# An order by hand on ScalarE, a chunk's writes and the expert loads behind the gathers, and low parts on GpSimd

## Chip, cores and metric

The kernel runs on one core of one Trainium2 chip. The metric is device time in microseconds (us), the median of three runs. The core has five engines that matter here: PE (TensorE, matrix products), ACT (ScalarE), DVE (VectorE), POOL (GpSimd) and SP (SyncE, which here issues DMAs). Each works through its own queue in order, and they wait for each other by semaphores.

## What is computed

An attention with a cluster mask gives 1536 tokens of 512 numbers. A feed-forward block with a squared ReLU follows, and then a mixture of eight experts, each 512 to 1024 and back to 512, in which every token goes to at most one expert:

```python
h = np.maximum(x @ w_in, 0.0)
x = h * h @ w_out                                  # first block
do_compute = x @ w_skip > 0                        # tokens that are computed
xc = x[do_compute]
logits = xc @ w_gate
e_idx = np.argmax(logits, axis=1)
probs = softmax(logits)
gate_w = probs[np.arange(len(xc)), e_idx]
for e in range(8):
    h = np.maximum(xc[e_idx == e] @ w1[e], 0.0)
    y[e_idx == e] = gate_w[e_idx == e, None] * (h @ w2[e])
out = x.copy()
out[do_compute] = xc + y
```

## The kernel before

Tokens are held in 12 tiles of 128, and in 4 chunks `ch` of 3 tiles (384 tokens). Attention takes the first half of the span. The first block follows in four passes over its hidden size: `gemm1` (products in L248) makes `hps`, ScalarE takes relu (L255) and square (L256) of it, GpSimd rounds it to the high part `hh` (L134) and DVE subtracts for the low part `hl` (L258); `gemm2` (L1091) multiplies by `woh` and `wol`, and DVE adds the sum to the tile (L1099). Every operand is split into a high and a low part, and a product is three: high by high, low by high, high by low.

The routing starts before the last pass has ended. `early()` routes chunks 0 to 2, `late()` the last. `route` transposes the tiles (L823, copied by ScalarE to `xs`, L825), multiplies by the gate weights, takes the exponential on ScalarE (`ex`, L867), makes a one-hot `oh` of the best expert (L873), the rank of each token within its expert by products on PE (`rk`, L877), and from the exponentials the factor `gate` (L892 to L898), which `pay` (L900) combines with the one-hot. `ranks` compares ranks with slots (`so`, L915), `slots` makes the lists of tokens by products of `so` and `pay` (`sl`, L923, summed by DVE in L927 and L929), and `index` makes indices of them (L933).

The work of the second block is cut into nine units of 128 tokens. Units 0 and 1 belong to the fullest expert, which `choose()` (L937 to L949) finds from the counts of chunks 0 to 2: list A of unit 0 is gathered by `gather(0)` from `out` (GpSimd, L1021, `u<-out_dram,ixA`), list B of unit 1 by `gather(1)` when the last chunk is routed (`u<-xd,ixB`), the lists of the other seven by `gather(2)` and so on (`ixp`). `choose()` sets `pi`: the fullest expert is p = 0, and one of experts 0 and 1 is p = 1. `place` reads them into registers on SP, and `fetch` (L747) issues the weight loads: pieces of 512 KB, into seven staging buffers, `st` (three) and four that were tiles of x (`xc`). `half_weights` turns a piece into its high part on ScalarE (CAST, L765, `wih` or `woh`) and its low part by two subtractions (L769, `wil` or `wol`); a table by expert (ENG0, ENG1, ENG2) names the engines, 'av' for ScalarE and DVE, 'ap' for ScalarE and GpSimd. `parts` (L1029 to L1033) transposes 128 tokens and splits them (`xh`, `xl` or `hh`, `hl`); `g1` and `g2` are the two products of a unit, `products` (L1039) the loop in them, L1047 the relu between, `finish` (L1060, L1062) scales and scatters.

`base()` is the sequence of steps n on PE: n = 0 to 11 the last `gemm1`s, 12 to 23 the last `gemm2`, 24 to 27 `g1(0, 0)`, 28 to 31 `g1(0, 1)`, and so on. The table EVENTS says what is put before step n: 'e' is the next part of `early()`, 'l' of `late()`, 'c' the conversion of one weight piece, 'x' the transposes of unit 0's tokens. `between(gen, f)` runs f after the second step of gen. The order of the instructions of an engine is as written for the engines named in MANUAL (one set per stage; the stage here is the third), and set by a scheduler for the others. In the third stage PE and SP are so named. In this stage ScalarE's queue holds also two DMA issues for each tile of the last chunk, to `xd` (L819) and to `out` (L820); the second must come behind `gather(0)`, which reads `out`.

Of the kernel before, what the change touches and what calls it, by code (L numbers as in the profile page):

```python
# [10 lines left out]
I32 = mybir.dt.int32  # L11
AF = mybir.ActivationFunctionType
ALU = mybir.AluOpType
# [22 lines left out]
LOADAT = 7  # L36
PE, ACT, DVE, POOL, SP = (mybir.EngineType.PE, mybir.EngineType.Activation, mybir.EngineType.DVE,
                          mybir.EngineType.Pool, mybir.EngineType.SP)
EVENTS = ((1, 'e'), (2, 'e'), (3, 'e'), (4, 'e'), (8, 'e'), (11, 'e'), (12, 'c'), (13, 'e'), (15, 'c'),
          (16, 'cce'), (18, 'el'), (21, 'x'), (22, 'lcc'), (25, 'c'), (26, 'l'), (28, 'lc'), (30, 'l'), (34, 'll'))  # L40
ENG0 = ('av',) * 8
ENG1 = ('av',) * 8
ENG2 = ('av',) * 8
HOLD = 2
M0 = {DVE, PE, ACT, POOL}
AFTER = 0
PACE = 3
CLOSE = 0
MANUAL = ({PE, ACT, DVE, POOL}, {PE}, {PE, SP}, {PE})


@with_exitstack
def clustered_attention_moe(
# [685 lines left out]
    def stage(t):  # L739
        free.append(t[:, 0:1024].rearrange("p (c f) -> p c f", c=2))  # L740

    def fetch():

        while free and loads and loads[0][0] < len(e_reg):
            p, kind, n, c = loads.pop(0)
            st = free.pop(0)
            nc.sync.dma_start(out=st, in_=w_slice(e_reg[p], kind, n)[:, c:c + 2])  # L747
            loaded.append(st)
# [57 lines left out]
    sg, sgB, sgp, t2 = [rp.tile([128, 6, E], F32, name=nm) for nm in ("sg", "sgB", "sgp", "t2")]  # L806
    nc.vector.tensor_scalar(out=sg[:, 5], in0=rev8[:, 0], scalar1=-1.0, scalar2=float(E), op0=ALU.mult, op1=ALU.add)
    ixp, pi = [rp.tile([128, E], I32, name=nm) for nm in ("ixp", "pi")]
    sAB = [rp.tile([128, 6], F32, name=nm) for nm in ("sA", "sB")]
    gp = rp.tile([128, E], F32, name="gp")  # L810
    ixAB = [rp.tile([128, 1], I32, name=nm) for nm in ("ixA", "ixB")]
# [4 lines left out]
    def turn_x(T):  # L816

        q = nc.sync if T < NT - GT else nc.scalar
        q.dma_start(out=xdv[T // TT, T % TT], in_=x1[T])  # L819
        q.dma_start(out=outv[T // TT, T % TT], in_=x1[T])  # L820
        xps = ps_x.tile([128, KD, 128], F32, name="xps", tag="x")
        for c in range(KD):
            nc.tensor.transpose(out=xps[:, c], in_=x1[T][:, c * 128:(c + 1) * 128], identity=ident)  # L823
        xs_t[T] = rp.tile([128, KD, 128], F32, name="xs", bufs=3)
        nc.scalar.copy(out=xs_t[T], in_=xps)  # L825
# [6 lines left out]
    def route(ch):  # L832
# [52 lines left out]
            count(i + 1, GT + 1, ones16, spread(oh16[:, ch * GT + i], GT - i), stop=(i == GT - 1))  # L885
        if ch >= NC - 2:
            nc.vector.tensor_copy(out=cnt, in_=rk[:, GT])
        rke = rp.tile([128, GT, E], F32, name="rke")
        nc.vector.tensor_tensor(out=rke, in0=rk[:, 0:GT], in1=oh16[:, t_], op=ALU.mult)
        nc.vector.tensor_reduce(out=rank[:, t_], in_=rke, op=ALU.add, axis=AX.X)  # L890
# [46 lines left out]
    def choose():  # L937

        nc.vector.tensor_reduce(out=cmax, in_=cnt, op=ALU.max, axis=AX.X)
        nc.vector.tensor_scalar(out=full, in0=cnt, scalar1=cmax, scalar2=None, op0=ALU.is_equal)  # L940
        nc.vector.tensor_tensor(out=full, in0=full, in1=rev8[:, 0], op=ALU.mult)
        er = rp.tile([128, 1], F32, name="er")
        nc.vector.tensor_reduce(out=er, in_=full, op=ALU.max, axis=AX.X)
        nc.vector.tensor_scalar(out=full, in0=full, scalar1=er, scalar2=None, op0=ALU.is_equal)
        nc.vector.tensor_scalar(out=pi[:, 0:1], in0=er, scalar1=-1.0, scalar2=float(E), op0=ALU.mult, op1=ALU.add)
        nc.vector.tensor_scalar(out=pi[:, 1:2], in0=full[:, 1:2], scalar1=-1.0, scalar2=1.0,
                                op0=ALU.mult, op1=ALU.add)
        nc.vector.tensor_scalar_min(nA, cmax, 128.0)
        place(2)  # L949

    def place(n):
        while len(e_reg) < n:
            p = len(e_reg)
            e_reg.append(nc.sync.value_load(pi[0:1, p:p + 1], min_val=0, max_val=E - 1))
            if p == 0:
                fetch()

    def pick(i, sum):

# [5 lines left out]
    def early():  # L965

        for ch in range(NC - 1):
            while done[0] <= ch:
                yield
            yield from route(ch)  # L970
            so = ranks(ch)
            yield
            if ch == NC - 2:
                choose()
            slots(ch, sg, so)
            if ch == NC - 2:
                pick(0, sg)
                gather(0)
            if ch < HOLD:
                stage(xc[ch])  # L980
            if ch == NC - 2:
                so = ranks(0, nA)
            yield
        for ch in range(NC - 1):
            slots(ch, sgB, so)
            if ch < NC - 2:
                so = ranks(ch + 1, nA)
            yield

    def late():  # L990
# [3 lines left out]
        slots(NC - 1, sgB, so)  # L994
        pick(1, sgB)
        gather(1)
        for ch in range(HOLD, NC):
            stage(xc[ch])
        yield
# [6 lines left out]
            lists[p + 1] = (ixp[:, p:p + 1], gp[:, p:p + 1])  # L1006
        gather(2)
        nc.vector.tensor_copy(out=pi, in_=sgp[:, 5])
        place(E)
        yield  # L1010


# [4 lines left out]
    def gather(u):  # L1017

        xg = xgs[u % 3]
        nc.gpsimd.memset(xg, 0.0)  # L1020
        nc.gpsimd.indirect_dma_start(  # L1021
            out=xg, in_=xd if u else out, in_offset=bass.IndirectOffsetOnAxis(ap=lists[u][0], axis=0),
            out_offset=None, bounds_check=N - 1, oob_is_err=False)
# [159 lines left out]
    for u in range(1, UN):  # L1183
# [9 lines left out]
        do(g1(u, 1) if u > 1 else between(g1(u, 1), lambda: turn_h(u, 0)))  # L1193
        if u + 1 < UN:
            xp_t[u + 1] = parts(xgs[(u + 1) % 3], "x")
        do(g2(u, 0))
        turn_h(u, 1)
    do(g2(UN - 1, 1))
    finish(UN - 1)

# [65 lines left out]
```

## Time and profile before

| | us |
|---|---|
| median of three runs | 683.02 |
| lowest and highest | 680.4, 685.97 |
| the profiled execution's own time | 684.3 |
| its span | 682.5 |
| PE busy in it | 648.4 (95%) |
| DVE, ACT, POOL busy in it | 477.4 (70%), 415.7 (61%), 253.7 (37%) |

The span is the time from the first to the last instruction that the profile saw; the rest of the execution lies around it. In the rows, a time in the front column is counted from the span's start, the next number is the duration, and the bracket at a row's end says how long the engine had been idle, and what ended that. PE, DVE, ACT, POOL are engines, PEq, ACTq and so on their instruction queues. [...]

### The profile page before, as it was taken

Reading aid. Unit: us, or ns where it says so; the run is one execution under the profiler, and the core shown is the slowest. Engines: PE = TensorE matmul, PEld = TensorE weight load, DVE = VectorE, ACT = ScalarE, POOL = GpSimd, SP = SyncE. Lnnn points to the kernel's source line nnn. Section 1 sums busy time; section 2 is a strip of 40 time slices with the busy share of each in tenths; the row PEclk is TensorE's granted clock in tenths of the full one; section 3 lists DMA queues with packets and bytes.
Section 4 is the critical chain, followed back from the end, with each engine's and each line's share of the span. In section 5 each row is a group of like instructions: output and inputs, shape, how many; then the busy total and the mean of one; then the engine's idle time right before and its main releaser. Section 6 shows DMA issues by size and latency. Waiting matters only on the chain. (4 is left out here: it accounts for less than half of the span.)

```text
span 682.5 us, 11258 instructions
## 1 busy us (share of the span) xinstructions
PE 648.4 (95%) x3769; PEld 566.0 (83%) x3769; DVE 477.4 (70%) x928; ACT 415.7 (61%) x846; POOL 253.7 (37%) x329
## 2 busy tenths in 40 slices
PE   7899899999999998999999999999999797999994
PEld 6788888989898887999998999999888575888883
DVE  4787899999999999654456455522244688899950
ACT  5799889989998984544433333322323375778830
POOL 4816264544736346643343443511010103113110
PEclk9899999999999999999999999999999989999998
DMA  5867764665746100123122312101222697999900
GB/s 130 190 150 154 185 142 122 150 157 127 164 123 139 41 1 9 63 66 104 63 78 62 108 63 62 40 0 47 93 93 94 216 315 252 345 356 362 367 13 23
DMA packets 72034, 89.90 MB, mean 132 GB/s; under 512 B 32384, under 2 KB 43584, under 8 KB 71968
## 3 DMA queue, kind: packets, MB, share of 16 engines
q1 hardware_dynamic: 68096, 84.12, 42.5%
q0 software_dynamic: 1440, 3.01, 1.3%
q10 hardware_dynamic: 2432, 1.97, 0.9%
q8 instruction: 32, 0.52, 0.3%
q14 instruction: 34, 0.28, 0.1%
HBM read 62.18 MB, written 9.44 MB: 105 GB/s over the span
## 5 line engine op out<-in xcount | busy, mean ns | idle before, releaser
L578 DVE TENSOR_TENSOR pl<-pt,ph 128x384 fp32r<-128x384 f32 x192 | 103.5, 551 | 19.2 <-ACT ph L569 18.0
L255 ACT ACTIVATE r<-hps 128x384 f32<-128x384 f32 x62 | 30.5, 492 | 120.7 <-PE hps L248 115.7
L555 PE MATMUL pt<-ident,p 128*128 128x128 f32 x576 | 95.9, 276 | 3.9 <-DVE pl L578 2.8
L513 PE MATMUL sc<-B,A 80*128 80x384 f32 (+1 forms) x384 | 91.8, 361 | 2.0 <-ACT p L529 1.8
L569 ACT CAST ph<-pt 128x384 fp32r<-128x384 f32 x192 | 89.7, 481 | 6.6 <-PE pt L555 5.9
L520 DVE TENSOR_REDUCE nm<-sc 128x1 f32<-128x768 f32 x96 | 91.0, 948 | 2.5 <-PE sc L513 2.5
L258 DVE TENSOR_TENSOR hl<-r,hh 128x384 fp32r<-128x384 f32 x62 | 36.7, 591 | 76.4 <-POOL hh L134 76.0
L529 ACT ACTIVATE p<-sc,nm 128x768 f32<-128x768 f32 x96 | 87.3, 910 | 4.4 <-DVE nm L520 4.3
L555 PEld LDWEIGHTS pt<-ident,p 128*128 128x128 f32 x576 | 70.4, 141 | 18.3 <-DVE pl L578 10.9
L134 POOL TENSOR_SCALAR hh<-r 128x384 fp32r<-128x384 f32 x62 | 35.4, 571 | 134.3 <-ACT r L256 114.9
L1091 PE MATMUL acc<-woh,hh 128*128 128x512 f32 x186 | 74.3, 400 | 0.0
L1091 PE MATMUL acc<-wol,hh 128*128 128x512 f32 x186 | 73.5, 395 | 0.0
L588 PE MATMUL av<-ph,vs 128*128 128x384 f32 x192 | 73.0, 380 | 0.1
L1091 PE MATMUL acc<-woh,hl 128*128 128x512 f32 x186 | 72.9, 392 | 0.0
L513 PEld LDWEIGHTS sc<-B,A 80*128 80x128 f32 (+1 forms) x384 | 63.2, 191 | 6.3 <-ACT p L529 6.2
L588 PE MATMUL av<-pl,vs 128*128 128x384 f32 x192 | 65.2, 339 | 0.6 <-DVE pl L578 0.6
L248 PE MATMUL hps<-A,wil 128*128 128x384 f32 x184 | 61.9, 336 | 2.0 <-POOL wil L180 2.0
L248 PE MATMUL hps<-A,wih 128*128 128x384 f32 x184 | 62.4, 339 | 0.0
L248 PE MATMUL hps<-B,wih 128*128 128x384 f32 x184 | 61.9, 337 | 0.0
L164 ACT ACTIVATE u<-st 128x512 f32<-128x512 f32 x32 | 21.7, 677 | 32.9 <-DMA st<-in_moe_w_in_dram 25.6
L1091 PEld LDWEIGHTS acc<-woh,hl 128*128 128x128 f32 x186 | 35.2, 189 | 7.8
L1091 PEld LDWEIGHTS acc<-woh,hh 128*128 128x128 f32 x186 | 35.2, 189 | 5.7 <-DVE xc L1099 0.2
(260 smaller groups left out, 1484.1 us busy)
## 6 DMA issues: line engine op xcount, KB each, us to landing
xc<-in_moe_w_dram SPq DMA_DIRECT2D x34, 512.0 KB, 5.5
st<-in_moe_w_dram SPq DMA_DIRECT2D x30, 512.0 KB, 5.8
st<-in_moe_w_in_dram SPq DMA_DIRECT2D x64, 128.0 KB, 2.9
st<-in_moe_w_out_dram SPq DMA_DIRECT2D x16, 512.0 KB, 3.9
A<-hi SPq DMA_DIRECT2D x30, 192.0 KB, 3.5
B<-hi SPq DMA_DIRECT2D x30, 192.0 KB, 4.0
qn<-in_q_dram SPq DMA_DIRECT2D x16, 192.0 KB, 3.5
vn<-in_v_dram SPq DMA_DIRECT2D x16, 192.0 KB, 2.6
```

What stands on the lines that cost most here:

```text
L134: nc.gpsimd.tensor_scalar(out=o, in0=i, scalar1=1.0, scalar2=0.0, op0=ALU.mult, op1=ALU.add)
L248: nc.tensor.matmul(out=hps, lhsT=wi[w][:, c, f * 128:(f + 1) * 128], rhs=xhl[ch][a][:, c], start=(n == 0), stop=(n == 3 * KD - 1))
L255: nc.scalar.activation(out=r, in_=hps, func=AF.Relu)
L258: nc.vector.tensor_tensor(out=hl, in0=r, in1=hh.bitcast(F32), op=ALU.subtract)
L513: nc.tensor.matmul(out=sc[:, c, 0:384], lhsT=A[h][0:kk, a, t * 128:(t + 1) * 128], rhs=Bk[h][0:kk, a, c * 384:(c + 1) * 384], start=(a == ...
L520: nc.vector.tensor_reduce(out=nm_t[i], in_=sc_t[i][:, :, 0:384], op=ALU.max, axis=AX.XY, negate=True)
L529: nc.scalar.activation(out=p, in_=sc[:, :, 0:384], func=AF.Exp, bias=nm, scale=1.0, accum_out=su_t[n, c][:, t, h:h + 1])
L555: nc.tensor.transpose(out=pt[:, c], in_=p_t[i][:, n, c * 128:(c + 1) * 128], identity=ident)
L569: nc.scalar.copy(out=block(i, n)[by_pool].bitcast(F32) if by_pool else block(i, n)[0], in_=pt_t[i, n])
L578: nc.vector.tensor_tensor(out=pl, in0=pt_t.pop((i, n)), in1=ph.bitcast(F32), op=ALU.subtract)
L588: nc.tensor.matmul(out=av, lhsT=vs[:, c, 2 * h:2 * h + 2].rearrange("p x d -> p (x d)"), rhs=r[:, c], start=(c == 0 and i == 0), stop=(c = ...
L1091: nc.tensor.matmul(out=acc, lhsT=h2[a][:, i * 128:(i + 1) * 128], rhs=wo[w][:, f], start=(f == 0 and n == 0), stop=(f == NF - 1 and n == 2))
```

## The change

EVENTS is laid out anew, with the weight pieces and unit 0's transposes at other steps. ScalarE is named in the third stage's MANUAL set. The eight subtractions of the second expert's first weights (p = 1, w1) are on GpSimd (ENG1). The writes of the last chunk to `out` go from ScalarE's queue to SP's, after `gather(1)`. `choose()` moves ahead of the rank and gate work of its chunk. It sets only the first expert's register and issues up to two loads; the second expert's number goes through GpSimd behind `gather(0)` (`pi1`), and the other loads are issued after that. In the last unit the transposes of the first half of `hs` stand between the products of `g2`. Lines of the kernel after are 1 to 13 further on.

```diff
--- before.py
+++ after.py
@@ -36,17 +36,18 @@
 LOADAT = 7
 PE, ACT, DVE, POOL, SP = (mybir.EngineType.PE, mybir.EngineType.Activation, mybir.EngineType.DVE,
                           mybir.EngineType.Pool, mybir.EngineType.SP)
-EVENTS = ((1, 'e'), (2, 'e'), (3, 'e'), (4, 'e'), (8, 'e'), (11, 'e'), (12, 'c'), (13, 'e'), (15, 'c'),
-          (16, 'cce'), (18, 'el'), (21, 'x'), (22, 'lcc'), (25, 'c'), (26, 'l'), (28, 'lc'), (30, 'l'), (34, 'll'))
+EVENTS = ((1, 'e'), (2, 'e'), (3, 'e'), (4, 'e'), (8, 'e'), (11, 'e'), (13, 'e'), (16, 'e'), (18, 'el'), (20, 'c'),
+          (21, 'c'), (22, 'l'), (23, 'c'), (24, 'xc'), (26, 'l'), (27, 'c'), (28, 'l'), (29, 'c'), (30, 'l'), (32, 'c'),
+          (33, 'c'), (34, 'll'))
 ENG0 = ('av',) * 8
-ENG1 = ('av',) * 8
+ENG1 = ('ap',) * 4 + ('av',) * 4
 ENG2 = ('av',) * 8
 HOLD = 2
 M0 = {DVE, PE, ACT, POOL}
 AFTER = 0
 PACE = 3
 CLOSE = 0
-MANUAL = ({PE, ACT, DVE, POOL}, {PE}, {PE, SP}, {PE})
+MANUAL = ({PE, ACT, DVE, POOL}, {PE}, {PE, SP, ACT}, {PE})
 
 
 @with_exitstack
@@ -739,9 +740,10 @@
     def stage(t):
         free.append(t[:, 0:1024].rearrange("p (c f) -> p c f", c=2))
 
-    def fetch():
-
-        while free and loads and loads[0][0] < len(e_reg):
+    def fetch(n=len(loads)):
+
+        while free and loads and loads[0][0] < len(e_reg) and n:
+            n -= 1
             p, kind, n, c = loads.pop(0)
             st = free.pop(0)
             nc.sync.dma_start(out=st, in_=w_slice(e_reg[p], kind, n)[:, c:c + 2])
@@ -806,6 +808,7 @@
     sg, sgB, sgp, t2 = [rp.tile([128, 6, E], F32, name=nm) for nm in ("sg", "sgB", "sgp", "t2")]
     nc.vector.tensor_scalar(out=sg[:, 5], in0=rev8[:, 0], scalar1=-1.0, scalar2=float(E), op0=ALU.mult, op1=ALU.add)
     ixp, pi = [rp.tile([128, E], I32, name=nm) for nm in ("ixp", "pi")]
+    pi1 = rp.tile([128, 1], I32, name="pi1")
     sAB = [rp.tile([128, 6], F32, name=nm) for nm in ("sA", "sB")]
     gp = rp.tile([128, E], F32, name="gp")
     ixAB = [rp.tile([128, 1], I32, name=nm) for nm in ("ixA", "ixB")]
@@ -817,7 +820,8 @@
 
         q = nc.sync if T < NT - GT else nc.scalar
         q.dma_start(out=xdv[T // TT, T % TT], in_=x1[T])
-        q.dma_start(out=outv[T // TT, T % TT], in_=x1[T])
+        if T < NT - GT:
+            q.dma_start(out=outv[T // TT, T % TT], in_=x1[T])
         xps = ps_x.tile([128, KD, 128], F32, name="xps", tag="x")
         for c in range(KD):
             nc.tensor.transpose(out=xps[:, c], in_=x1[T][:, c * 128:(c + 1) * 128], identity=ident)
@@ -885,6 +889,8 @@
             count(i + 1, GT + 1, ones16, spread(oh16[:, ch * GT + i], GT - i), stop=(i == GT - 1))
         if ch >= NC - 2:
             nc.vector.tensor_copy(out=cnt, in_=rk[:, GT])
+        if ch == NC - 2:
+            choose()
         rke = rp.tile([128, GT, E], F32, name="rke")
         nc.vector.tensor_tensor(out=rke, in0=rk[:, 0:GT], in1=oh16[:, t_], op=ALU.mult)
         nc.vector.tensor_reduce(out=rank[:, t_], in_=rke, op=ALU.add, axis=AX.X)
@@ -946,14 +952,13 @@
         nc.vector.tensor_scalar(out=pi[:, 1:2], in0=full[:, 1:2], scalar1=-1.0, scalar2=1.0,
                                 op0=ALU.mult, op1=ALU.add)
         nc.vector.tensor_scalar_min(nA, cmax, 128.0)
-        place(2)
-
-    def place(n):
+        place(1, pi)
+        fetch(2)
+
+    def place(n, src):
         while len(e_reg) < n:
             p = len(e_reg)
-            e_reg.append(nc.sync.value_load(pi[0:1, p:p + 1], min_val=0, max_val=E - 1))
-            if p == 0:
-                fetch()
+            e_reg.append(nc.sync.value_load(src[0:1, 0:1] if n == 2 else src[0:1, p:p + 1], min_val=0, max_val=E - 1))
 
     def pick(i, sum):
 
@@ -970,12 +975,15 @@
             yield from route(ch)
             so = ranks(ch)
             yield
-            if ch == NC - 2:
-                choose()
             slots(ch, sg, so)
             if ch == NC - 2:
                 pick(0, sg)
                 gather(0)
+
+                nc.gpsimd.tensor_scalar(out=pi1, in0=ixAB[0], scalar1=0.0, scalar2=None, op0=ALU.mult)
+                nc.gpsimd.tensor_tensor(out=pi1, in0=pi1, in1=pi[:, 1:2], op=ALU.add)
+                place(2, pi1)
+                fetch()
             if ch < HOLD:
                 stage(xc[ch])
             if ch == NC - 2:
@@ -994,6 +1002,8 @@
         slots(NC - 1, sgB, so)
         pick(1, sgB)
         gather(1)
+        for T in range(NT - GT, NT):
+            nc.sync.dma_start(out=outv[T // TT, T % TT], in_=x1[T])
         for ch in range(HOLD, NC):
             stage(xc[ch])
         yield
@@ -1006,7 +1016,7 @@
             lists[p + 1] = (ixp[:, p:p + 1], gp[:, p:p + 1])
         gather(2)
         nc.vector.tensor_copy(out=pi, in_=sgp[:, 5])
-        place(E)
+        place(E, pi)
         yield
 
 
@@ -1193,8 +1203,11 @@
         do(g1(u, 1) if u > 1 else between(g1(u, 1), lambda: turn_h(u, 0)))
         if u + 1 < UN:
             xp_t[u + 1] = parts(xgs[(u + 1) % 3], "x")
-        do(g2(u, 0))
-        turn_h(u, 1)
+        if u + 1 < UN:
+            do(g2(u, 0))
+            turn_h(u, 1)
+        else:
+            do(between(g2(u, 0), lambda: turn_h(u, 1)))
     do(g2(UN - 1, 1))
     finish(UN - 1)
 
```

On ScalarE, at the end of the last gemm1, the relu and square of the first block (L255 and L256, after: L256 and L257), the exponential of the third chunk (ex) and the first weight casts (wih) stood like this before:

```order
L255 ACTIVATE r<-hps 128x384
L256 ACTIVATE r<-r 128x384
L867 ACTIVATE ex<-ex 128x24
L255 ACTIVATE r<-hps 128x384
L256 ACTIVATE r<-r 128x384
L255 ACTIVATE r<-hps 128x384
L256 ACTIVATE r<-r 128x384
L819 DMA xd<-xc_91 128x512
L765 CAST wih<-st 128x1024
L820 DMA out_dram<-xc_91 128x512
L765 CAST wih<-st 128x1024
L825 COPY xs<-xps 128x512
```

and stand like this after:

```order
L256 ACTIVATE r<-hps 128x384
L257 ACTIVATE r<-r 128x384
L256 ACTIVATE r<-hps 128x384
L257 ACTIVATE r<-r 128x384
L871 ACTIVATE ex<-ex 128x24
L256 ACTIVATE r<-hps 128x384
L257 ACTIVATE r<-r 128x384
L822 DMA xd<-xc_91 128x512
L829 COPY xs<-xps 128x512
L767 CAST wih<-st 128x1024 x2
L822 DMA xd<-xc_91 128x512
L829 COPY xs<-xps 128x512
```

The exponential stands one relu and one square later, and between the casts now stand copies of xs and no write to `out`.

On DVE, the chain from the exponential's first reader (gate) to pay of the third chunk began like this before (pay comes eight instructions after these):

```order
L892 TENSOR_REDUCE gate<-ex 128x3
L873 TENSOR_TENSOR oh_3989<-oh_6475,sel 128x24
L893 TENSOR_SCALAR gate<-gate 128x3
L903 TENSOR_TENSOR cum_3990<-cum_3990,oh_3989 128x8
L258 TENSOR_TENSOR hl<-r,hh 128x384
L894 RECIPROCAL gate<-gate 128x3
L903 TENSOR_TENSOR cum_3990<-cum_3990,oh_3989 128x8
L896 CAST vals<-gate 128x3
L903 TENSOR_TENSOR cum_3990<-cum_3990,oh_3989 128x8
L898 TENSOR_TENSOR gate<-gate,vals 128x3
L887 COPY cnt<-rk 128x8
L889 TENSOR_TENSOR rke<-rk,oh_3989 128x24
```

and begins like this after (pay comes eight instructions after these, too):

```order
L898 TENSOR_REDUCE gate<-ex 128x3
L918 TENSOR_SCALAR rkb<-rank,nA 128x3
L259 TENSOR_TENSOR hl<-r,hh 128x384
L949 TENSOR_REDUCE er<-full 128x1
L899 TENSOR_SCALAR gate<-gate 128x3
L921 TENSOR_TENSOR so<-slot,rkb 128x384
L950 TENSOR_SCALAR full<-full,er 128x8
L951 TENSOR_SCALAR pi<-er 128x1
L900 RECIPROCAL gate<-gate 128x3
L952 TENSOR_SCALAR pi<-full 128x1
```

The next step of gate now stands behind an hl, and the reciprocal behind a comparison (so) and the small instructions of choose().

On GpSimd, around the gathers of list A (ixA) and list B (ixB), hh being the last high parts of the first block, the order was this before:

```order
L1020 MEMSET u 128x512
L134 TENSOR_SCALAR hh<-r 128x384 x21
L1021 DMA u<-out_dram,ixA 128x512
L1021 DMA u<-xd,ixB 128x512
L1021 DMA l_5821<-xd,ixp 128x512
```

and is this after (pi is the second expert's number, wil the low parts of the second expert's w1):

```order
L135 TENSOR_SCALAR hh<-r 128x384 x20
L1031 DMA u<-out_dram,ixA 128x512
L983 TENSOR_SCALAR pi_4007<-ixA 128x1
L135 TENSOR_SCALAR hh<-r 128x384
L984 TENSOR_TENSOR pi_4007<-pi_4007,pi 128x1
L771 TENSOR_TENSOR wil<-xc_88,wih 128x512 x2
L771 TENSOR_TENSOR wil<-xc_89,wih 128x512 x2
L771 TENSOR_TENSOR wil<-st,wih 128x512 x3
L1031 DMA u<-xd,ixB 128x512
L1031 DMA l_5822<-xd,ixp 128x512
L771 TENSOR_TENSOR wil<-st,wih 128x512
```

One hh of the first block moved behind the first gather's issue, and seven subtractions stand ahead of the second gather.

On PE, around unit 0's transposes (xps<-ident,u) and its first products (hps<-wih,xh), the order was this before:

```order
L1091 MATMUL acc<-wol,hh 128x512
L1091 MATMUL acc<-woh,hl 128x512
L1029 MATMUL xps<-ident,u 128x128 x4
L1091 MATMUL acc<-woh,hh 128x512
L1091 MATMUL acc<-wol,hh 128x512
L1091 MATMUL acc<-woh,hl 128x512
L823 MATMUL xps<-ident,xc_91 128x128 x4
L829 MATMUL lps<-wgs,xs 128x9 x4
L1091 MATMUL acc<-woh,hh 128x512
L1091 MATMUL acc<-wol,hh 128x512
L1091 MATMUL acc<-woh,hl 128x512
L1091 MATMUL acc<-woh,hh 128x512
```

and is this after:

```order
L833 MATMUL lps<-wgs,xs 128x9 x4
L1101 MATMUL acc<-woh,hh 128x512
L1101 MATMUL acc<-wol,hh 128x512
L1101 MATMUL acc<-woh,hl 128x512
L1101 MATMUL acc<-woh,hh 128x512
L1101 MATMUL acc<-wol,hh 128x512
L1101 MATMUL acc<-woh,hl 128x512
L1039 MATMUL xps<-ident,u 128x128 x4
L1049 MATMUL hps<-wih,xh 128x512
L1049 MATMUL hps<-wil,xh 128x512
L1049 MATMUL hps<-wih,xl 128x512
```

The transposes of u moved behind the last products of the first block, directly ahead of the first products that read them.

## Rows read from the trace of the kernel before

**Rows 1.** The page's second part: granted clock of PE in 40 slices of the span.

```profile
PEclk9899999999999999999999999999999989999998
```

**Rows 2.** Waits of PE from 500 us on: total, times, longest.

```profile
PE xps L1029 <- DMA u<-out_dram,ixA: 2.8, 1, 2.8
PE acc L1039 <- ACT hh L1032: 2.6, 2, 1.9
PE sl L923 <- DVE pay L900: 1.5, 2, 1.0
PE hps L1039 <- ACT xh L1032: 0.7, 1, 0.7
PE xps L823 <- ACT xs L825: 0.6, 1, 0.6
```

**Rows 3.** Windows of 4 us: length, busy time of each engine, clock, DMA share, GB/s.

```profile
544.00:548.00 4.00, 3.40 (x16) 2.97 (x15) 3.30 (x6) 4.00 (x7) 0.00 (x0) 0.63 1.04 378
548.00:552.00 4.00, 4.00 (x11) 3.08 (x11) 2.60 (x5) 2.45 (x3) 0.00 (x0) 0.52 0.98 349
...
560.00:564.00 4.00, 2.51 (x14) 1.55 (x14) 4.00 (x15) 3.17 (x5) 0.00 (x0) 1.00 0.91 314
```

**Rows 4.** Timeline of PE: start, duration, engine, line, operation, idle time before.

```profile
532.11 0.24 PE L923 MATMUL sl<-pay,so 128*128 128x40 bf16 x3 [0.56 <-DVE pay L900]
...
558.48 0.17 PE L877 MATMUL rk<-oh,tri 128*128 128x24 bf16 x1 [0.49 <-DVE oh L873]
...
579.28 0.50 PE L1039 MATMUL acc<-woh,hh 128*128 128x512 f32 x1 [1.89 <-ACT hh L1032]
...
670.53 0.50 PE L1039 MATMUL acc<-woh,hh 128*128 128x512 f32 x1 [0.68 <-ACT hh L1032]
```

**Rows 5.** Timeline of ACT (ScalarE), same columns.

```profile
528.56 0.21 ACT L867 ACTIVATE ex<-ex 128x24 f32<-128x24 f32 x1
...
530.38 0.53 ACT L256 ACTIVATE r<-r 128x384 f32<-128x384 f32 x1
...
543.48 1.05 ACT L765 CAST wih<-st 128x1024 fp32r<-128x1024 f32 x1 [4.23 <-DMA u<-out_dram,ixA]
...
555.29 0.60 ACT L1047 ACTIVATE hs<-hps 128x512 f32<-128x512 f32 x1 [0.74 <-PE hps L1039]
...
562.66 0.59 ACT L1032 CAST hh<-xps 128x512 fp32r<-128x512 f32 x1
...
577.70 1.05 ACT L765 CAST wih<-st 128x1024 fp32r<-128x1024 f32 x1 [2.12 <-DMA st<-in_moe_w_dram]
```

**Rows 6.** Timeline of DVE (VectorE), same columns.

```profile
531.47 0.59 DVE L900 TENSOR_TENSOR pay<-oh,vals 128x120 bf16<-128x120 bf16 x1
...
533.08 0.55 DVE L915 TENSOR_TENSOR so<-slot,rkb 128x384 bf16<-128x384 f32 x1
```

**Rows 7.** Timeline of POOL (GpSimd), same columns.

```profile
530.98 0.94 POOL L134 TENSOR_SCALAR hh<-r 128x384 fp32r<-128x384 f32 x1 [1.74 <-ACT r L256]
534.13 0.51 POOL L134 TENSOR_SCALAR hh<-r 128x384 fp32r<-128x384 f32 x1 [2.21 <-ACT r L256]
535.26 1.56 POOL L1021 DMA_INDIRECT u<-out_dram,ixA  x1 [0.61 <-DVE hl L258]
565.56 1.38 POOL L1021 DMA_INDIRECT u<-xd,ixB  x1 [28.74 <-DMA xc<-in_moe_w_dram]
```

**Rows 8.** Lines L180 and L769, the subtractions: min, median, max in ns.

```profile
L180 POOL TENSOR_TENSOR wil<-u,wih x16: 1279/1311/1712, 94.9 to 431.7; 128x512 fp32r<-128x512 f32 x16
...
L769 DVE TENSOR_TENSOR wil<-xc,wih x34: 667/681/694, 547.8 to 646.3; 128x512 fp32r<-128x512 f32 x34
```

**Rows 9.** Timeline of GpSimd and DVE, where they meet and where not.

```profile
371.33 1.31 POOL L180 TENSOR_TENSOR wol<-u,woh 128x512 fp32r<-128x512 f32 x1
...
371.66 1.26 DVE L166 TENSOR_SCALAR u<-u 128x512 f32<-128x512 f32 x1
...
400.23 0.42 DVE L166 TENSOR_SCALAR u<-u 128x512 f32<-128x512 f32 x1
```

## The prediction

> **What bounds the kernel.** I read the page's first two parts first: PE is busy 95% of the span (table above), so what counts is where it waits or runs slowly. The granted clock [rows 1] is at or near full everywhere but in the slice from 546 to 563 us. The waits of PE from 500 us to the end [rows 2] list the stalls there: 2.8 us for the gathered tokens u (list A), 2.6 for hh (two waits), 1.5 for pay (two), 0.7 for xh, 0.6 for xs. [...]
>
> So the region 528 to 582 us decides, and the end of the last unit. All times below are against the profiled execution, 684.3 us with a span of 682.5, some 1.3 above the median of 683.02; I apply differences to the median.
>
> **What the change removes.** (1) The transposes of u go behind the rest of the last gemm2 on PE (the order fence on PE), nine products and another tile's transposes later: the 2.8 us [rows 2] go. (2) ScalarE's write to `out` waited on the gather at its queue's head; the cast behind it shows 4.23 us of idle time, ended by u [rows 5]. It held xs, for which PE waited 0.6; with the write on SP this goes. (3) The clock: if its fall follows the gather's stall, 3.2 us. (4) The 1.89 us before 579.28: there a cast of weights waited 2.12 us for its load and stood ahead of hh [rows 5]; the new ScalarE order has hh ahead of that cast. (5) The last unit's transposes of hs move between the products of gemm2, where the 0.68 us before 670.53 [rows 4] and a shorter wait behind it go: 0.8 as an estimate. Sum: 2.8 + 0.6 + 3.2 + 1.9 + 0.8 = 9.3 us.
>
> **What it adds.** (a) ScalarE's exp for the third chunk now stands behind one more relu and square (order fence on ScalarE). Before, it began at 528.56, and the square ahead of which it stood ended at 530.91 [rows 5]: exp ends near 531.1 instead of 528.77, 2.36 later. Its readers, gate to pay, were through at 532.06 [rows 6], 3.3 us behind it, as the last of 20 DVE instructions. Now 18 stand there, and the third is an hl that waits for GpSimd's hh, which ended at 531.92 [rows 7]; gate's chain goes on behind it (order fence on DVE). From 531.92: hl and one comparison at 0.55 [rows 6], 13 small ones at some 0.1, an estimate, and pay 0.3 give 534.6. PE waits for pay at 532.11 already [rows 4], so the delay of 2.6 us is all new stall: 2.6 (1.9, if other work hid the small ones, to 3.3).
> (b) On GpSimd the gather's issue, 1.56 us [rows 7], and two small instructions now stand ahead of the last hh of the last gemm1, which began at 534.13 before it. I take 0.2 us off for slack, an estimate: 1.35 (0 to 1.6).
> (c) The transposes of u stand directly ahead of the first products that read xh and xl. The same pattern for the second list costs 0.7 us for xh [rows 2]; xl is a subtraction of 0.68 [rows 8] behind others on DVE, another 1.1 (0 to 1.4): 1.85.
> (d) The last chunk's one-hot now stands on DVE behind the first two subtractions of w2 and hl. Their cast follows hs on ScalarE. From hs at 555.29 (0.60 us [rows 5]): cast 1.05, two subtractions 1.3, four small ones 0.6, hl 0.6, oh 0.2 gives 559.7; PE got rk at 558.48 [rows 4]: 1.2 (0 to 1.5).
> (e) gather(1) stands behind seven of GpSimd's eight subtractions (order fence on GpSimd). The last of their casts stands behind hh, which began at 562.66 [rows 5]: 562.66 + 0.59 + 1.05, one more cast 1.05, one subtraction 1.31 [rows 8] is 566.65, against an issue at 565.56 [rows 7]: 1.1 (0 to 2).
> (f) Weight loads: the second and later ones now wait on SP for a register that GpSimd makes behind the gather's issue, so they start some 5 us later, an estimate from (a) and the 1.56. The casts of g1(0,0)'s pieces should still come 1 to 2 us before PE reaches them: nothing; if that cover is gone, 1 to 2 us. The out-writes on SP stand behind gather(1), between loads that run a unit ahead: nothing.
> Sum: 2.6 + 1.35 + 1.85 + 1.2 + 1.1 = 8.1. Without more, the change gains 1.2 us.
>
> **GpSimd's subtractions.** One 128x512 subtraction takes 1.31 us on GpSimd and 0.68 on DVE [rows 8], and eight leave DVE. But one instruction of DVE's that met such a subtraction took 1.26 us instead of 0.42 (371.66 against 400.23, with the GpSimd row at 371.33 [rows 9]): it was held 0.84. Seven of the eight fall between the last chunk's logits and ixB, where PE waits for DVE's chain (1.5 us for pay already [rows 2]). The lower bound is 0: the freed 8 x 0.68 us of DVE could even repay it. The upper is their whole length, 7 x 1.31 = 9.2. I take four that hold something for which PE waits: 4 x 0.84 = 3.4, about half of the seven, since the chain itself stops for PE and ScalarE between its parts. Then -1.2 + 3.4 = +2.2: **685.2 us**.
>
> [...]
>
> **Rivals.**
> B, as designed: the waits go and (a), (b), (d), (e) are hidden, only (c) stays: -9.3 + 1.85 = -7.4, 675.6. For it: every removed stall stands in a row. Against: DVE is busy all of 560 to 564 [rows 3], so a later exp or a later cast is late for PE.
> [...]
> D, the clock falls somewhere else: the gap made by (a) is 0.56 + 2.6 = 3.2 us, longer than the 2.8 that came before the fall, while 1.89 had none. Then the 3.2 stay lost: 685.2 + 3.2 = 688.4.
> E, it does not do what it says: the counter of fetch is overwritten inside its loop, so fetch(2) issues one load where two were named. No stall hangs on that second load before the gather, so this leaves the time at the forecast's.
>
> **Numbers.** Chances: forecast with E 0.42, B 0.20, C 0.18, D 0.20. A measurement of this kernel tells about 1% (6.8 us) from no change. Faster than 676.2: most of B, 0.16, and 0.01 of the rest, 0.17. Slower than 689.9: 0.09 of C, 0.09 of D, 0.07 of the forecast's own spread, 0.25. Same: 0.58. The forecast's own range is 681 to 689; with half of B and most of C the range is 676 to 691.
>
> **What would show it.** Right: no wait for u<-out_dram; a wait for pay of about 3.2 us near 532; waits for hh of GpSimd and for xh of the first unit; rk and sl waits of over 2 us together with GpSimd's subtractions, and DVE instructions of the chain at 0.8 us and more beside them; the acc wait of 1.89 and the end's 0.68 gone. Wrong: pay no later than before (the exp term), a full clock through 528 to 560 with waits under 4 us in sum (B), or two slices at a clock under 0.8 (D).

## The result and the profile after

The changed kernel took 694.09 us (median of four runs, 691.34 to 696.09) against 683.31 for the kernel before (median of four, too): the ratio is 1.0148, with a 95% interval of 1.0116 to 1.0179. It is slower by 1.5%, and above the range of the prediction. The profiled execution took 691.34 us with a span of 689.6, 7.0 more than the one of before; it is the quickest of the four.

The waits of PE from 500 us to the end, after (total, times, longest):

```profile
PE sl L929 <- DVE pay L906: 7.7, 2, 4.6
PE rk L881 <- DVE oh L877: 1.7, 1, 1.7
PE rk L881 <- DVE sel L876: 1.5, 1, 1.5
PE hps L1049 <- ACT xh L1042: 1.4, 2, 0.7
PE hps L1049 <- DVE xl L1043: 0.9, 2, 0.7
PE acc L1101 <- POOL hh L135: 0.7, 1, 0.7
```

Of the rows of before [rows 2] the waits for u of list A, for hh from ScalarE and for xs are gone, as forecast. In their place stand 7.7 us for pay and 3.2 for rk. Before, beside the rows shown ahead, the chain of the last chunk cost PE only this (same view, kernel before):

```profile
PE rk L877 <- DVE oh L873: 0.5, 1, 0.5
PE sl L923 <- DVE sgB L929: 0.5, 1, 0.5
PE xps L1029 <- DMA u<-xd,ixB: 0.4, 1, 0.4
```

The timeline of PE shows where the waits lie:

```profile
535.23 0.24 PE L929 MATMUL sl<-pay,so 128*128 128x40 bf16 x3 [3.07 <-DVE pay L906]
...
539.10 0.50 PE L1101 MATMUL acc<-woh,hh 128*128 128x512 f32 x1 [0.74 <-POOL hh L135]
...
548.88 0.50 PE L1049 MATMUL hps<-wih,xh 128*128 128x512 f32 x1 [0.68 <-ACT xh L1042]
...
560.31 0.17 PE L881 MATMUL rk<-oh,tri 128*128 128x24 bf16 x1 [1.65 <-DVE oh L877]
...
570.08 0.28 PE L929 MATMUL sl<-pay,so 128*128 128x40 bf16 x3 [4.64 <-DVE pay L906]
...
677.65 0.40 PE L1049 MATMUL acc<-woh,hl 128*128 128x512 f32 x1
```

The first wait for pay (3.07 us at 535.23) belongs to the third chunk, and answers to the 0.56 at 532.11 [rows 4]. The one of 4.64 belongs to the last chunk. The 1.89 us ahead of 579.28 and the 0.68 ahead of 670.53 of before [rows 4] have no counterpart any more. The last product ends at 678.05, before at 673.85:

```profile
673.46 0.39 PE L1039 MATMUL acc<-woh,hl 128*128 128x512 f32 x1
```

The windows of 4 us (busy time of PE, PEld, DVE, ACT, POOL, then the granted clock as a share of the full one, DMA share, GB/s):

```profile
536.00:540.00 4.00, 3.25 (x16) 1.90 (x14) 1.95 (x8) 1.01 (x2) 2.15 (x4) 1.00 0.52 173
...
560.00:564.00 4.00, 3.69 (x14) 2.98 (x14) 3.97 (x12) 1.85 (x3) 3.43 (x2) 0.66 0.05 18
564.00:568.00 4.00, 1.43 (x7) 0.90 (x6) 4.00 (x9) 2.74 (x4) 2.81 (x2) 0.92 0.97 316
568.00:572.00 4.00, 1.50 (x9) 1.22 (x10) 4.00 (x18) 0.00 (x0) 2.20 (x3) 0.51 0.38 142
572.00:576.00 4.00, 4.00 (x13) 3.14 (x12) 0.65 (x8) 1.04 (x1) 3.08 (x3) 0.64 0.28 76
```

Before, the clock was 0.63 and 0.52 at 544 to 552 [rows 3]. After, it is 1.00 in both of these windows and below 1 from 560 to 576. What was lost is, as an estimate, the busy time by the missing share: 3.69 x 0.34 + 1.43 x 0.08 + 1.50 x 0.49 + 4.00 x 0.36 = 3.5 us.

DVE's chain of the last chunk, after, and GpSimd's subtractions beside it (both timelines; the first number is the start, the second the duration):

```profile
557.10 1.25 DVE L870 SCALAR_TENSOR_TENSOR oh<-ex,rev 128x24 f32<-128x24 f32 x1
...
562.76 0.17 DVE L896 TENSOR_REDUCE rank<-rke 128x3 f32<-128x24 f32 x1
562.85 1.16 DVE L902 CAST vals<-gate 128x3 bf16<-128x3 f32 x1
...
564.65 0.17 DVE L902 CAST vals<-gate 128x3 bf16<-128x3 f32 x1
...
565.26 1.76 DVE L771 TENSOR_TENSOR wol<-st,woh 128x512 fp32r<-128x512 f32 x1
566.94 1.23 DVE L902 CAST vals<-gate 128x3 bf16<-128x3 f32 x1
...
568.68 1.33 DVE L906 TENSOR_TENSOR pay<-oh,vals 128x120 bf16<-128x120 bf16 x1
```

```profile
556.88 2.65 POOL L771 TENSOR_TENSOR wil<-xc,wih 128x512 fp32r<-128x512 f32 x2 [17.69 <-ACT wih L767]
560.56 3.43 POOL L771 TENSOR_TENSOR wil<-xc,wih 128x512 fp32r<-128x512 f32 x2 [1.03 <-DVE gate L899]
565.19 4.69 POOL L771 TENSOR_TENSOR wil<-st,wih 128x512 fp32r<-128x512 f32 x3 [1.20 <-ACT wih L767]
```

A step of the one-hot (oh) took 1.25 us, a cast of three numbers a partition (vals) 1.16 and 1.23, a subtraction 1.76 instead of 0.68 [rows 8], pay 1.33. Each began while GpSimd was in a subtraction; the same cast at 564.65, when GpSimd was in none, took 0.17. The reduction at 562.76 began beside a subtraction, too, and took 0.17, so not every instruction beside a subtraction took longer. GpSimd's subtractions took longer in turn, 1.7 us each in the second pair (3.43 for two) instead of 1.31 [rows 8].

The last difference stands at the end. From the page of the profile, before and after, the span and the packets of the second queue that it calls "instruction" (q14):

```profile
span 682.5 us, 11258 instructions
...
q14 instruction: 34, 0.28, 0.1%
```

```profile
span 689.6 us, 11269 instructions
...
q14 instruction: 35, 0.29, 0.1%
```

And the wait of SP's queue for PE's at the last line of the program (the waits of SP from 670 us on), before and after:

```profile
SPq L1261 <- PEq L1261: 3.0, 2, 2.5
```

```profile
SPq L1274 <- PEq L1274: 5.7, 2, 5.1
```

Before, the last product ended at 673.85 and the span 8.65 us later; after, at 678.05 and 11.55 us later. So 2.9 of the 7.0 us come behind the last product.

### The profile page after: what moved, and what is told of

Its sections match the earlier page's. It is cut to its first block, busy times and chain, and to the rows that moved or that the text cites. A ratio compares the mean times of both kernels' runs of the same rounds, so it can differ in the third digit from the quotient of the medians.

```text
span 689.6 us, 11269 instructions
## 1 busy us (share of the span) xinstructions
PE 648.2 (94%) x3769; PEld 565.3 (82%) x3769; DVE 480.9 (70%) x920; ACT 416.4 (60%) x846; POOL 263.5 (38%) x339
## 5 line engine op out<-in xcount | busy, mean ns | idle before, releaser
L256 ACT ACTIVATE r<-hps 128x384 f32<-128x384 f32 x62 | 30.4, 491 | 126.1 <-PE hps L249 118.7
L556 PEld LDWEIGHTS pt<-ident,p 128*128 128x128 f32 x576 | 70.0, 140 | 18.5 <-DVE pl L579 10.8
```

The costliest lines, as they stand in the source:

```text
L256: nc.scalar.activation(out=r, in_=hps, func=AF.Relu)
L556: nc.tensor.transpose(out=pt[:, c], in_=p_t[i][:, n, c * 128:(c + 1) * 128], identity=ident)
```

## The experiments

All ratios are to the kernel before, run beside the kernel on the same chip, with 95% intervals; the times of different experiments come from different chips, so ratios are compared.

**e1: low parts back on DVE.** The kernel after with

```diff
-ENG1 = ('ap',) * 4 + ('av',) * 4
+ENG1 = ('av',) * 8
```

> The kernel after with p=1's eight low-part subtractions of w1 back on DVE. Theory 1 (GpSimd's subtractions hold DVE's rank chain): the waits of 1.47 and 1.65 us for rk shrink to about 1.5 together, the 4.64 us for the last chunk's pay to 1 to 1.5, and the half-speed stretches behind them (some 3.4 us lost at 561 to 575) go; in all 6 to 9 us: 685 to 688. Theory 2 (what costs is ScalarE's order by hand, with exp and the casts late, and the later loads): the waits stay within 1 us of what they are, 692 to 695.

Measured: 688.63 us beside 685.19 for before, 1.0049 (1.0016 to 1.0081). The last chunk's wait for pay gave way to one of 1.44 us for sgB; rk cost 2.4 us instead of 3.1, and 2.69 us for u of list B came in. So by the ratios GpSimd's part of the loss is 0.9 to 1.0%, and half a per cent is left. This part holds the subtractions that run and those in a loop that doesn't; e5 parts the two. The slow stretches did not go, as theory 1 expected: in this profile the clock was 0.50 from 536 to 540, behind a wait of 3.08 us for the third chunk's pay, and 0.50 from 576 to 580, behind the wait for list B.

**e2: the same subtractions in the kernel before**, ENG1 as in after, nothing else.

> The kernel before with only the eight subtractions moved to GpSimd. Theory 1: rk and pay waits grow by 3 to 6 us around 556 to 570, and the clock may fall a second time there: 687 to 692. Theory 2: no change within 2 us of 683.3, or a gain of up to 2 since DVE is relieved.

Measured: 693.38 us, 1.0128 (1.0091 to 1.0165). This one line, which also reaches the loop that doesn't run, loses nearly as much as the whole change. Theory 2 falls as the main cause.

**e3 and e4: ScalarE's order left to the scheduler**, in after and in e1's kernel.

```diff
-MANUAL = ({PE, ACT, DVE, POOL}, {PE}, {PE, SP, ACT}, {PE})
+MANUAL = ({PE, ACT, DVE, POOL}, {PE}, {PE, SP}, {PE})
```

> The kernel after with ScalarE's order left to the scheduler again in that stage (all else as after). [...] Theory 2: nearly the whole loss goes, 683 to 687.

> Both undone: subtractions on DVE and ScalarE's order left to the scheduler; what is left is the new EVENTS, choose() early, the loads and out-writes behind the gathers and the end's transposes. Theory 1: about 681 to 685, the waits for u and for the casts gone and the chain's waits small. Theory 2: the same as e3 within 1 us, 683 to 687.

Measured: e3 693.57 us, 1.0127 (1.0092 to 1.0162); e4 683.94 us, 0.9994 (0.9964 to 1.0024). With GpSimd's subtractions the order by hand makes no difference that shows; without them it costs, by the ratios, the half per cent that e1 had left, though the two intervals overlap. e3's profiled execution (686.64 us) lies far from its other four (692.28 to 693.93), so its waits say little of them; the third chunk's pay waited 1.59 us in it. What remains of the change in e4 (EVENTS, choose() early, loads and writes behind the gathers, the end) is worth nothing on balance: its profile has no wait for u of list A, but 2.40 us for xh, 1.92 for rk and 1.19 for GpSimd's hh.

**e5: the skipped loop as before.** These inputs never enter the loop for overfull experts, but the loop holds p = 1's conversions too, so the change had put 64 subtractions there on GpSimd. The kernel after with

```diff
-                (nc.vector if eng[1] == "v" else nc.gpsimd).tensor_tensor(
+                (nc.vector if eng[1] == "v" or src is not None else nc.gpsimd).tensor_tensor(
```

> The kernel after, with the low parts on DVE only in the loop for overfull experts, which these inputs skip: GpSimd has 64 instructions fewer to jump over, and nothing else changes. In the kernels with GpSimd's subtractions the span ends 11.2 to 11.6 us behind PE's last product, in those without 8.6. Theory 3 (the longer skipped code costs one more fetch of instructions at the end): the end comes 8.6 us behind the last product, 2.9 less than after: about 691. Rival (the tail is chance, or belongs to the scatter): 11.5 us, the time as after, 694.

Measured: 688.95 us, 1.0053 (1.0019 to 1.0087). The last product ended at 677.99 and the span at 686.6: 8.6 us, as theory 3 says. By the ratios the gain, 0.8 to 1.0%, is more than the 2.9 us of the tail. No executed instruction differs, yet in this profile the last chunk's pay took 0.28 us, though GpSimd had three subtractions from 567.22 on (timelines of DVE and GpSimd, then of PE):

```profile
567.84 0.28 DVE L906 TENSOR_TENSOR pay<-oh,vals 128x120 bf16<-128x120 bf16 x1
```

```profile
567.22 4.55 POOL L771 TENSOR_TENSOR wil<-st,wih 128x512 fp32r<-128x512 f32 x3 [1.93 <-ACT wih L767]
```

```profile
568.18 0.24 PE L929 MATMUL sl<-pay,so 128*128 128x40 bf16 x3 [1.66 <-DVE pay L906]
```

The wait was 1.66 instead of 4.64: pay took 0.28 and the cast ahead of it (at 567.17) 0.17 here, 1.33 and 1.23 in after. It brought nothing in this profile, since 2.04 us for u of list B came in and the last product ended with after's to 0.06 us: the 3.0 us between the two profiled executions are the tail alone. What the rest of the gain in the ratio is stays open. Beside e1 (1.0049), which has none of these subtractions on GpSimd, run or not, e5's 1.0053 says one thing more: in the kernel after, the eight subtractions that run cost nothing that could be told within these intervals (0.3% to each side), and what e1 gained goes with the code that is not run.

**e6: the exponential earlier.** After, with the third chunk's exp one relu and square earlier on ScalarE:

```diff
+        if ch == NC - 2:
+            yield
         rk = ps_l.tile([128, GT + 1, E], F32, name="rk", tag="l")
```

(and one more 'e' in EVENTS, at step 6).

> The kernel after with one more stop in route, so that the third chunk's exp stands on ScalarE one relu and square earlier, as before the change; PE's and GpSimd's order is as after. If exp's place makes the first pay wait: it falls from 3.07 to under 1 us, and 2 to 2.5 us go: about 691.5. If choose() ahead of gate on DVE makes it: it stays over 2 us, 694.

Measured: 691.36 us, 1.0062 (1.0045 to 1.0079). PE's timeline:

```profile
539.32 0.24 PE L931 MATMUL sl<-pay,so 128*128 128x40 bf16 x3 [1.61 <-DVE pay L908]
...
543.62 0.49 PE L1103 MATMUL acc<-woh,hh 128*128 128x512 f32 x1 [1.18 <-POOL hh L135]
```

The wait fell from 3.07 to 1.61 us, not under 1: about half belongs to exp's place. In the rest, choose()'s instructions and one more hl now stand between gate and pay on DVE; no run moves choose() alone, so that it is theirs is not shown. Part went into a longer wait for hh. The ratio is 0.7 to 0.9% below that of after, more than these waits account for; the last chunk's pay still cost 5.19 us there, so the interval and the chain's chance may carry the rest. It stays open.

**e7 and e8: parts of the change alone in the kernel before.** e7 moves the last unit's transposes between its products and the out-writes to SP; e8 also moves unit 0's transposes to step 24.

```diff
-EVENTS = ... (18, 'el'), (21, 'x'), (22, 'lcc'), (25, 'c') ...
+EVENTS = ... (18, 'el'), (22, 'lcc'), (24, 'x'), (25, 'c') ...
```

> The kernel before with only the last unit's transposes moved between the products, and the last chunk's out-writes on SP behind gather(1). Theory: the wait of 0.68 us at the end and that of 0.60 for xs go, the casts of the first weights start earlier, the waits for u and for hh stay: 1 to 2 us faster than before, ratio 0.997. Rival (the freed ScalarE only shifts the stall into the wait for u): 0 to 1 us.

> The same with the transposes of u at step 24 as in after, and the weight pieces where before has them. If moving the transposes takes the wait for u away without a new one: that wait 0, xh and xl waits of 1.4 to 2.4, and if the clock's fall follows the gap for u it goes too: 4 to 6 us faster than before, ratio 0.992 to 0.994. If the clock falls all the same and xh and xl take the gain: within 1 us of the kernel without it.

Measured: e7 684.81 us, 0.9974 (0.9948 to 1.0001); e8 688.08 us, 1.0014 (0.9984 to 1.0043). e7's profile lost the two waits it was to lose, and has 3.61 us for u and 3.30 for rk. In e8 the wait for u is gone and one of 3.43 for xh stands at 549.23 instead, and the clock was 0.50 to 0.74 from 548 to 564. Moving the consumer behind other work moved the stall to the next consumer; the two ratios' intervals overlap.

**e9: skipped code alone.** The kernel before with 64 subtractions on GpSimd in the loop that is not entered; in the executed part every engine's order is that of before.

```diff
-                (nc.vector if eng[1] == "v" else nc.gpsimd).tensor_tensor(
+                (nc.vector if src is None or kind else nc.gpsimd).tensor_tensor(
```

> The kernel before with 64 subtractions put on GpSimd in the loop for overfull experts alone, which these inputs skip: not one executed instruction differs from before. Theory 3 (skipped code costs a fetch at the end): the span ends 11.5 us behind PE's last product instead of 8.6, and the ratio is 1.004 (2.9 of 685). Rival: 8.6 us and a ratio within 0.001 of 1.

Measured: 689.36 us, 1.0065 (1.0038 to 1.0092). The last product, the page's rows, and SP's wait at the end:

```profile
672.96 0.39 PE L1039 MATMUL acc<-woh,hl 128*128 128x512 f32 x1
```

```profile
span 684.4 us, 11258 instructions
...
q14 instruction: 35, 0.29, 0.1%
```

```profile
SPq L1261 <- PEq L1261: 5.5, 2, 4.9
```

As many instructions ran as before (11258), the last product ended at 673.35, before's time to half a microsecond, and the span 11.05 us later; there is one packet more on q14. In each of the seven profiles with the extra code for GpSimd in that loop (after, e2, e3, e6, e9, e11, e15) the tail is 11.0 to 11.7 us, in each of the eleven without it 8.6 to 8.8. The packets of q14, in the fourteen of these profiles whose page gives them, are 34 in the nine without the code and 35 in the five with it, but for e15 with 36. So the code goes with 2.4 (e9) to 2.9 us (after) of tail and with one packet more; that the packet fills this time, no row shows. By the ratio e9 lost some 4.4 us, 2 more than its tail; what these are stays open.

**e10: the executed subtractions alone.** The kernel before with ENG1 of after and e5's line.

> The kernel before with GpSimd's eight subtractions in the executed part alone, the skipped loop as before. Theory 1 (the rank chain on DVE is held): what e2 showed without its tail, ratio 1.0075 to 1.010, tail 8.6 us, waits for oh and pay of 2 to 4 us each. Rival, which e5 and e1 suggest by their nearly equal ratios (the held chain costs nearly nothing, the tail and chance are the rest): 1.000 to 1.004.

Measured: 690.87 us, 1.0106 (1.0070 to 1.0142), tail 8.6 us. PE's timeline:

```profile
559.83 0.17 PE L877 MATMUL rk<-oh,tri 128*128 128x24 bf16 x1 [2.60 <-DVE oh L873]
...
568.65 0.28 PE L923 MATMUL sl<-pay,so 128*128 128x40 bf16 x3 [3.68 <-DVE pay L900]
```

Against 0.49 for rk [rows 4] and 0.96 for pay before, the chain costs 4.8 us more, and the clock fell to 0.67 and 0.52 behind these two gaps. Theory 1 stands in the kernel before; in the kernel after, e1 and e5 give its subtractions no price of their own. e9's and e10's prices add to 1.7%, e2's is 1.28: within the intervals the two make up the third.

**e11 and e12: after once more, and its subtractions on another matrix.** e12 puts the second expert's w2 on GpSimd instead of w1 (ENG1 = ('av',) * 4 + ('ap',) * 4, and e5's line).

> The kernel after, unchanged, beside the others: if its ratio is 1.013 to 1.016 as first measured, e5's gain of over 0.9% is more than its 2.9 us of tail, and GpSimd's meeting with pay (4.64 us against 1.66 in e5's profile) is the rest. If it is near 1.0095, e5's gain is the tail alone.

> The kernel after with GpSimd doing the low parts of the second expert's w2 instead of w1: as many subtractions, but behind gather(1) and the last chunk's rank chain, and the skipped loop on DVE. If what costs is the place (the chain), it is as e1, ratio 1.003 to 1.006, with waits for pay and oh like e1's. If the number costs, 1.009 or more.

Measured: e11 693.8 us, 1.0136 (1.0103 to 1.0168), which repeats the first result; e12 689.71 us, 1.0085 (1.0060 to 1.0109). e12's profile has e1's waits (3.08, 1.44, 2.55 us) and a span of 687.7 against e1's 687.6, but its ratio lies between the two expectations: place against number is not settled by it.

**e13 and e14: filling the gaps.** e13 is the kernel before with ten extra products ahead of unit 0's transposes; their result is overwritten. e14 is e7 with eleven there and eight ahead of the last chunk's rank products.

```diff
+        for _ in range(fill):
+            w = wparts[steps[-1][0]][1][0]
+            nc.tensor.matmul(out=tps, lhsT=w[:, 0, 0:128], rhs=w[:, 0], start=True, stop=True)
         for c in range(4):
             nc.tensor.transpose(out=tps[:, c], in_=src[:, c * 128:(c + 1) * 128], identity=ident)
```

> The kernel before with ten extra products of 128x512 on PE ahead of unit 0's transposes (their result is overwritten): at 0.23 us each they fill 2.3 of the 2.8 to 3.6 us in which PE waited for u. If the half speed at 545 to 551 follows PE's idle time, it goes, and the time falls by about 3 us, ratio 0.995 to 0.997. If it follows something else, it stays, and the ratio is 0.999 to 1.002.

> e7's kernel with eleven such products ahead of unit 0's transposes and eight ahead of the last chunk's rank products, where its profile shows waits of 3.61 and 3.30 us, each followed by a slower stretch. If the slow stretches follow the idle time, both go and with them 3 to 6 us: ratio 0.990 to 0.994, faster than both kernels. If not, 0.996 to 1.000 as e7.

Measured: e13 684.15 us, 0.9984 (0.9957 to 1.0011); e14 682.32 us, 0.9968 (0.9948 to 0.9989). e13's timeline of PE and windows:

```profile
539.49 2.43 PE L1030 MATMUL xps<-woh 128*128 128x512 f32 x10
543.02 0.66 PE L1032 MATMUL xps<-ident,u 128*128 128x128 f32 x4 [1.10 <-DMA u<-out_dram,ixA]
```

```profile
544.00:548.00 4.00, 3.40 (x22) 2.71 (x20) 3.41 (x6) 4.00 (x7) 0.00 (x0) 1.00 0.98 361
548.00:552.00 4.00, 3.30 (x21) 2.65 (x20) 4.00 (x8) 3.45 (x5) 0.00 (x0) 1.00 0.98 349
```

The wait for u is 1.10 us instead of 2.8, and the stretch that ran at 0.63 and 0.52 before [rows 3] runs at 1.00. So at this place the fall does follow the idle time; over the twelve runs the mean clock was 0.987 to 0.995, against 0.980 to 0.993 for before beside them. But in the profile a later fall came (0.77 and 0.80 at 576 to 584, where PE stood idle for 1.33 us of the first window), and the ratio doesn't part from 1. In e14 no window is below 1.00:

```profile
544.00:548.00 4.00, 3.61 (x24) 3.26 (x25) 3.00 (x5) 2.82 (x4) 0.00 (x0) 1.00 1.05 407
548.00:552.00 4.00, 3.84 (x24) 3.06 (x23) 3.72 (x7) 2.85 (x5) 0.00 (x0) 1.00 1.05 391
...
560.00:564.00 4.00, 2.74 (x19) 2.09 (x19) 4.00 (x15) 2.29 (x4) 0.00 (x0) 1.00 1.03 368
```

It is the one kernel faster than both, by 0.3% against the kernel before; 0.6 to 1.0% was expected. How much of that is the products' and how much e7's edits, the two ratios don't tell; the clock is the products'.

**e15 and e16: the same in after and in e4**, eight products ahead of rk and five ahead of the last chunk's sl.

> The kernel after with eight extra products on PE ahead of the last chunk's rank products (waits of 1.47 and 1.65 us in its profile) and five ahead of its sl products (4.64 us); no other engine's order differs. If a fall of the clock follows idle time: the slow stretch at 561 to 565 (1.6 us lost) goes, the one behind the longer gap may stay; 1.5 to 3 us less, ratio 1.009 to 1.012 instead of 1.0136 to 1.0148. If not: 1.013 or more.

> e4's kernel with the same extra products (eight and five): its times were near 682.4 where the mean clock was 0.99 and near 688 where it was 0.98. If the falls follow idle time, most runs come near 682, ratio 0.995 to 0.998, about as e14. If not, as e4, 0.999 to 1.001.

Measured: e15 692.84 us, 1.0134 (1.0098 to 1.0170); e16 684.85 us, 0.9996 (0.9972 to 1.0021). e15's timeline of PE and windows:

```profile
535.52 0.24 PE L937 MATMUL sl<-pay,so 128*128 128x40 bf16 x3 [3.08 <-DVE pay L908]
```

```profile
536.00:540.00 4.00, 4.00 (x16) 2.99 (x15) 2.22 (x9) 1.01 (x2) 2.16 (x4) 0.60 0.52 172
...
560.00:564.00 4.00, 3.33 (x21) 2.77 (x20) 3.97 (x8) 2.03 (x4) 3.61 (x3) 1.00 0.19 74
...
568.00:572.00 4.00, 2.17 (x10) 1.75 (x11) 4.00 (x23) 1.04 (x1) 1.89 (x2) 0.50 0.74 270
572.00:576.00 4.00, 4.00 (x14) 3.17 (x13) 0.35 (x4) 1.05 (x1) 2.77 (x3) 0.71 0.28 82
```

The fall behind the rank products (0.66 in after) is gone, the one behind the remaining 4.03 us for pay stayed. The place is as expected, the time is not less by what can be measured. One reason stands in the first window: behind the third chunk's 3.08 us, which had no fall in after's profile, the clock was 0.60, and the whole loss by the clock is 4.0 us against 3.5. e16 fell to 0.50 behind a gap of 1.86 us for xh that I had not filled, and is as e4.

## Why the prediction was wrong

**What held.** The terms for waits were near. (a) pay of the third chunk: 3.07 - 0.56 = 2.5 us, forecast 2.6; e6 shows that exp's place is somewhat over half of it. (b) hh: 0.74, forecast 1.35. (c) xh and xl: 0.68 + 0.74 = 1.4, forecast 1.85. (d), (e) and GpSimd's subtractions together, 5.7 in the forecast: rk and sl of the last chunk cost 1.47 + 1.65 + 4.64 + 0.42 = 8.2 us against 0.5 + 1.0 + 0.5 for rk, pay and sgB and 0.4 for list B before, 5.8 more. That this sum fits is in part luck: in e1's profile, with none of these subtractions on GpSimd, the same chain cost 0.40 + 2.02 + 1.44 and 2.69 for list B, 6.6 us. So in after the new order alone makes some 4.2 of it, where (d) and (e) had 2.3, and the subtractions the other 1.6, where I had 3.4; in the kernel before the same subtractions made the chain 4.8 longer (e10). The upper of 9.2 (C in the chances) was too much in both: not each instruction of the chain that met a subtraction took longer, since the reduction at 562.76 took 0.17. The removals (1), (2) and (5) came as forecast. The 1.89 us of (4) are gone, too, but e9, with the order of before on every engine, doesn't have them either, so this is not shown to be the new order's work. (f) cost nothing: no wait for the first weights is in the list.

**The first step that failed is (3), the clock.** I counted 3.2 us of slow running as a gain: PE's busy time in the two windows from 544 [rows 3] by the missing share of the clock, 3.40 x 0.37 + 4.00 x 0.48, an estimate. The reading was that the fall follows the gap of 2.8 us for u [rows 2]; behind the 1.89 ahead of 579.28 [rows 4] there was none (1.00 from 576 to 584). At that place the reading was right (1.00 in e13 with 1.10 us for u), and that is why the gain could not come: the change takes one gap away and makes others. After lost 3.5 us at 560 to 576, so the term was 0.3 on the wrong side instead of -3.2. Rival D had this price, with another place: it expected the fall behind the 3.2 us gap for the third chunk's pay. There the clock stayed at 1.00 in the profiles of after and of e11, but e1, e5, e12 and e15 have the same gap of 3.1 us, and each fell behind it: to 0.50 (e1) and 0.60 (e15) in the window from 536, and to 0.75 (e12) and 0.90 (e5) in the one from 540. So D's place counts in some executions, and the clock is a term with a spread that one profile doesn't give. What I should have done is count the gaps of (a), of (d) and of the subtractions as gaps, too. I also overlooked in [rows 1] that the second slice (17 to 34 us) stands at 8, in a stretch that the change doesn't touch: before's clock was 0.86 from 20 to 30 us there, after's 1.00, and in e11's page of the same kernel after the slice stands at 8 again.

**The second is a step that was not there.** Nothing in the prediction read the code that is skipped, though the table ENG1 holds for the loop of overfull experts too. It costs 2.9 us of tail in the profile (8.65 to 11.55), and 2.4 shown alone by e9.

With both, the sum is 2.2 + 3.5 + 2.9 - 0.1 - 0.6 - 0.4 + 0.1 = 7.6 us against 7.0 measured in the profiled executions. The medians differ by 10.8: after's profiled execution is the quickest of its four, 2.8 below its median, and before's was 1.0 above. What made the other three slower no trace shows; their mean clock was 0.979 to 0.982, against 0.986 in the profiled one.

**What stays open.** Why the same 3.1 us of waiting for pay brought a fall of the clock in four profiles and none in two, and 1.86 us did in e16 where 1.89 did not before: the length of a gap alone doesn't tell. Why by their ratios e5 gained, and e9 lost, more than the tail. And why the subtractions that run cost 1% in the kernel before and nothing measurable in the kernel after.

## What to carry to other kernels

Before moving elementwise work to GpSimd, look at what DVE does in the same microseconds: a chain of tiny instructions for which PE waits is a bad neighbour, since some of them took 1.16 to 1.33 us beside a subtraction here, where 0.17 and 0.28 were measured too. What that costs depends on what else the chain waits for: 1.0106 in the kernel before (e10), nothing that could be told in the kernel after (e5 beside e1). A gap of PE costs twice when the clock falls behind it (before: 2.8 us for u and, as an estimate, 3.2 at 0.63 and 0.52), so a stall that is only moved can keep both prices (e8: 3.43 us for xh, then 0.50 to 0.74), and the gain of a full clock may be booked only if no other gap is made. A constant that sets engines also sets them in code that is not entered, and such code alone made the tail 2.4 us longer (e9).

## What was not expected of the hardware

Useless products in a gap cost nothing that could be measured (0.9984 in e13, 0.9968 in e14) and the clock stayed up: with eleven and eight of them it was 1.00 from 536 to 584 us (e14), where e7 without them fell to 0.50 and 0.58. A kernel with sixty-four instructions more that never run was slower by 0.65% (0.38 to 0.92, e9), of which the tail of 2.4 us is about half. And a cast of 128 by 3 on DVE, 0.17 us alone, took 1.23 beside GpSimd's subtraction, while a reduction there (at 562.76) took 0.17; in e5 pay took 0.28 beside one, where it took 1.33 in after.
